# New ranks for the planned order of a three-stage float32 kernel, and softmax two blocks ahead in place of three

## The chip, the cores and the metric

One core of a Trainium2 chip runs the kernel. The metric is the device time of one execution in microseconds. Traces come from a profiled execution of their own.

## The reference

Eight batches (B = 8) of 576 tokens (S) pass through three stages, all in float32:

```
kv  = einsum('bhsd,bhse->bhde', k, v)              # 8 heads of 64
out = einsum('bhsd,bhde->bhse', q, kv)
x   = out / sqrt(mean(out*out, -1) + 1e-6) * g_norm       # (8, 576, 512)
w   = softmax over the top 2 of 4 of x @ w_gate
for e in 4 experts (64 wide):
    a  = softmax(causal(scale * (x @ wq[e]) @ (x @ wk[e]).T))
    y += mask_e * w_e * ((a @ (x @ wv[e])) @ wo[e])
h   = gelu(y @ w_in); u, v = h[..., :512], h[..., 512:]
v_s = einsum('ts,bsd->btd', w_sg, layernorm(v) * g_ln) + b_sg
out = y + (u * v_s) @ w_out
```

Below, "the attention" is the masked softmax attention of the four experts (called heads 0 to 3 in the text). What the kernel calls the first stage (q k v products, norm) feeds it.

## The kernel before, in words

Nearly every product of two float32 operands is made as three fast products: each operand is split in a high part (a rounding, on ScalarE) and a low part (a difference, on VectorE or GpSimd), and high x high, high x low and low x high are summed in PSUM.

The program is written in two phases. Phase 1 (class Phase1, from line 404) handles first stage and attention, batch by batch, and phase 2 (class Phase2, from line 1020) the last stage. Nothing is issued as it is written: a Recorder (line 208) keeps each operation with its tiles. Its plan (line 289) then walks a model of the five engines, and whenever an engine of the model is free it gives it the operation with the lowest number in the record, among those whose operands are ready and whose buffers are to be had. trace (line 377) issues everything in the order of the model's start times. So all instructions carry line 395, and the profile's groups are told apart by their tiles. On the chip each engine takes its instructions in that fixed order.

The numbers in the record come from merge (line 1006). Work is cut into streams (generators); each stream has a stretch of ranks, in units of a batch, from OPT["w"] (line 49). A stream's next step has the rank lo + (hi - lo) x (cost of its steps so far) / (its total), and merge always runs the step with the lowest rank. The streams of batch b (streams, line 981), all of them shifted by b:

- front (line 689): for four pairs of heads, kv, outT and stat (tiles kvps, outps, statps), then rstd (line 585; tiles ya, yb, yc, rr), the reciprocal roots.
- norm (normall, line 711): the products nps, the scaled tile o, and its halves xhi and xlo. There is one buffer for xhi and xlo, so norm of a batch follows the last q and k of the batch before.
- v (vpart, line 719): five tiles vps, and the gates (line 666). qk0 and qk1 (qkpart, line 731): q and k of heads 0, 1 and of heads 2, 3 (tiles qkps, hiT, loT); SyncE's DMAs then spread them into qs, kh and kl.
- attn (line 857): 20 blocks (4 heads x 5 row blocks). scores (line 738) makes scps on TensorE, adds the mask and takes the minimum on VectorE, and the exponential on ScalarE (tile prob, 4 buffers). transp (line 787) transposes block n - ahead (tile tps), and splits it into aTh and aTl; av (line 817) is the product with v.
- wts (line 499): 12 splits of the first stage's weights (wstage into whi and wlo), at the start alone.
- conv and conv2 (line 952): the last stage's weights are read, put together, split and stored to DRAM (tiles cv_*, wxps), in 16 + 27 units spread over the batches. Each unit has small operations on ScalarE, VectorE and GpSimd, and DMAs on SyncE's queue.
- u (Phase2.first, line 1229): loads, then the nine raw V tiles (vmat) and the four raw U tiles (upart) of the last stage's first batches (tiles ps, copied to vraw and u by ScalarE and VectorE). Their buffers come free only when all other streams of phase 1 but attn are done.

What follows in Phase2.rest (line 1249) has the highest numbers: vnorm (line 1155: gelu, the layer norm's statistics on VectorE, lny on GpSimd, the scaled tiles vg, vn and vhi), then spart and opart (tiles ps). The PSUM pools have 4 banks for attn and 4 for the rest; ps of V and U have 4.

Keys with _0 hold for batch 0 alone. The loops that the change touches through OPT:

```
def merge(first, others=()):
    live = [[lo, (hi - lo) / total, gen, True] for lo, hi, total, gen in first]
...
        t = min(live, key=lambda u: u[0])
        cost = next(t[2], 0)
...
            t[0] += t[1] * (cost or 1.0)
```

Of the kernel before, what the change touches and what calls it, by code (L numbers as in the profile page):

```python
# [45 lines left out]
HF = 288  # L46
BIG = 1.0e9
SMALL = float(np.array(897 << 20, np.uint32).view(np.float32))
OPT = dict(ob=1, sx=0, pinq=0, dv=0, pin=1, cvb=2, xb=1, ldb=2, hp={}, n1=0, n2=0, f1=0, pa=4, sA=(), dg=0, cost=(1.01, 0.88, 1.22, 1.47, 1.28), avi=1, prb=4, ahb=2, alb=2, qkb=2, ahead=3, w={'attn': (0.0, 1.0), 'qk1': (-0.013, 0.222), 'qk0': (-0.54, -0.204), 'v': (-0.683, -0.28), 'front': (-1.386, -0.923), 'norm': (-0.832, -0.787), 'conv': (0.032, 3.4), 'conv2': (3.4, 7.2), 'wts': (-1.938, -1.368), 'u': (0.25, 1.0), 'front_0': (-1.763, -1.646), 'v_0': (-1.478, -1.291), 'qk0_0': (-1.025, -0.914), 'qk1_0': (-0.003, 0.152), 'norm_0': (-1.6, -1.5)})


AFTER = {
# [351 lines left out]
class Phase1:  # L404
# [6 lines left out]
    def __init__(self, tc, late, early, ins, wts, gvd, nb):  # L411
# [4 lines left out]
        self.ac = right("ac", 1)  # L416
        self.qk = right("qk", OPT["qkb"])
        self.vv = right("vv", 2)
        self.at = right("at", 2)
        self.psa = right("psa", OPT["pa"], space=PSUM)  # L420
        self.cst = left("cst", 1)
        self.ld = left("ld", OPT["ldb"])
        self.xp = left("xp", 1)
        self.tmp = left("tmp", 1)
        self.cv = left("cv", OPT["cvb"])
        self.psp = left("psp", 7 + OPT["sx"] - OPT["pa"], space=PSUM)
        if not OPT["sx"]:
            self.aux = left("aux", 1, space=PSUM)
# [952 lines left out]
```

## Time and profile before

| what | value |
|---|---|
| median of 3 runs | 894.33 us (893.02 to 898.92) |
| the profiled execution, its own time | 893.27 us |
| its span, first to last instruction | 891.5 us |
| TensorE busy with matmuls | 853.2 us, 96% |
| VectorE, ScalarE, GpSimd busy | 512.4, 464.7, 350.8 us |
| mean granted TensorE clock | 0.980 |

Busy times are unions over the span; idle time of an engine is put down to what ended it. A granted clock of 1.00 is 2.4 GHz and 0.50 is 1.2 GHz. All stretches (A:B) are microseconds from the span's start. Phase 1 fills the first 528 us or so, phase 2 the rest.

### The profile page before, as it was taken

Reading aid. Unit: us, or ns where it says so; the run is one execution under the profiler, and the core shown is the slowest. Engines: PE = TensorE matmul, PEld = TensorE weight load, DVE = VectorE, ACT = ScalarE, POOL = GpSimd, SP = SyncE. Lnnn points to the kernel's source line nnn. Section 1 sums busy time; section 2 is a strip of 40 time slices with the busy share of each in tenths; the row PEclk is TensorE's granted clock in tenths of the full one; section 3 lists DMA queues with packets and bytes.
Section 4 is the critical chain, followed back from the end, with each engine's and each line's share of the span. In section 5 each row is a group of like instructions: output and inputs, shape, how many; then the busy total and the mean of one; then the engine's idle time right before and its main releaser. Section 6 shows DMA issues by size and latency. Waiting matters only on the chain.

```text
span 891.5 us, 16825 instructions
## 1 busy us (share of the span) xinstructions
PE 853.2 (96%) x5992; PEld 794.8 (89%) x5992; DVE 512.4 (57%) x1427; ACT 464.7 (52%) x1211; POOL 350.8 (39%) x398
## 2 busy tenths in 40 slices
PE   7799998999999999999999979999999999999998
PEld 4598997988989989988898769999999999999998
DVE  1757677788866787888878765633342423230110
ACT  1556676677766776867767765522242324231110
POOL 0284266485743644768622223313131413130210
PEclk9799998999999999999899989999999999999999
DMA  9378373674864956746435936020202020101011
GB/s 306 133 196 215 95 217 82 194 215 124 228 179 127 254 156 181 213 148 168 132 88 137 315 109 241 26 94 14 94 26 94 14 93 1 54 1 54 14 41 54
DMA packets 76262, 114.34 MB, mean 128 GB/s; under 512 B 12865, under 2 KB 40321, under 8 KB 76178
## 3 DMA queue, kind: packets, MB, share of 16 engines
q1 hardware_dynamic: 75938, 112.87, 43.0%
q8 instruction: 48, 0.79, 0.4%
q0 software_dynamic: 240, 0.39, 0.2%
q14 instruction: 36, 0.29, 0.1%
HBM read 58.14 MB, written 26.77 MB: 95 GB/s over the span
## 4 chain that ended last, share of the span: by engine, by line
PE 86%; DVE 8%; ACT 2%; issue 1%; DMA 1%; SPq 0%; POOL 0%; ACTq 0%; DVEq 0%; POOLq 0%
PE ps L395 42%; PE qkps L395 10%; PE vps L395 7%; PE avps L395 6%; PE scps L395 5%; PE tps L395 4%; PE kvps L395 4%; PE outps L395 3%; PE statps L395 2%; DVE aTl L395 1%; PE wxps L395 1%; DVE prob L395 1%; DVE o L395 1%; PE nps L395 1%; PE rps L395 1%
## 5 line engine op out<-in xcount | busy, mean ns | idle before, releaser
L395 PE MATMUL ps<-wsh,vn 128*128 128x288 f32 x576 | 119.7, 295 | 0.0
L395 ACT ACTIVATE prob<-prob,small 128x128 f32<-128x128 f32 (+4 forms) x160 | 96.6, 605 | 20.5 <-DVE small L395 18.1
L395 POOL TENSOR_TENSOR gl<-g,gh 128x576 fp32r<-128x576 f32 x32 | 45.8, 1432 | 134.3 <-ACT gh L395 134.2
L395 PEld LDWEIGHTS ps<-wsh,vn 128*128 128x128 f32 x576 | 94.3, 188 | 0.6
L395 DVE CUSTOM_DVE_ANT_0 prob<-scps,mask_sb 128x128 f32<-128x128 f32 (+4 forms) x160 | 75.2, 475 | 18.8 <-PE scps L395 17.5
L395 DVE TENSOR_TENSOR aTl<-tps,aTh 128x384 fp32r<-128x384 f32 (+1 forms) x192 | 79.9, 430 | 7.0 <-ACT aTh L395 5.3
L395 DVE TENSOR_TENSOR g<-ps,u 128x288 f32<-128x288 f32 x64 | 29.1, 454 | 86.7 <-PE ps L395 86.7
L395 ACT CAST aTh<-tps 128x384 fp32r<-128x384 f32 (+1 forms) x192 | 69.4, 380 | 17.8 <-PE tps L395 14.2
L395 PE MATMUL qkps<-xhi,whi 128*128 128x288 f32 x256 | 78.4, 306 | 0.1
L395 PE MATMUL tps<-id_sb,prob 96*128 96x96 f32 (+2 forms) x480 | 73.0, 261 | 3.8 <-DVE small L395 1.3
L395 PE MATMUL qkps<-xhi,wlo 128*128 128x288 f32 x256 | 75.8, 296 | 0.0
L395 PE MATMUL qkps<-xlo,whi 128*128 128x288 f32 x256 | 75.7, 296 | 0.0
L395 PE MATMUL ps<-wsl,vn 128*128 128x288 f32 x256 | 75.6, 295 | 0.0
L395 PE MATMUL ps<-gh,wo2l 128*128 128x288 f32 x256 | 75.4, 295 | 0.0
L395 PE MATMUL ps<-gl,wo2h 128*128 128x288 f32 x256 | 75.3, 295 | 0.0
L395 PE MATMUL ps<-gh,wo2h 128*128 128x288 f32 x256 | 75.3, 294 | 0.0
L395 POOL TENSOR_SCALAR lny<-mv 128x1 f32<-128x1 f32 x36 | 22.3, 620 | 131.7 <-DVE mv L395 131.3
L395 PE MATMUL scps<-kh,qs 128*128 128x128 f32 (+2 forms) x192 | 69.7, 368 | 4.4 <-DVE small L395 2.2
L395 POOL TENSOR_TENSOR xlo<-o,xhi 128x576 fp32r<-128x576 f32 x30 | 42.2, 1421 | 58.6 <-ACT xhi L395 58.6
L395 PEld LDWEIGHTS tps<-id_sb,prob 96*128 96x128 f32 (+2 forms) x480 | 52.3, 140 | 12.6 <-DVE small L395 2.2
L395 PE MATMUL avps<-aTh,vst 128*128 128x320 f32 (+4 forms) x224 | 61.8, 296 | 1.8 <-DVE aTl L395 1.3
L395 ACT COPY oev<-ps 128x288 f32<-128x288 f32 x32 | 12.7, 398 | 92.8 <-PE ps L395 92.8
(169 smaller groups left out, 2629.1 us busy)
## 6 DMA issues: line engine op xcount, KB each, us to landing
kv<-in_kvp SPq DMA_DIRECT2D x30, 384.0 KB, 5.1
kh<-hiT SPq DMA_DIRECT2D x64, 144.0 KB, 3.2
kl<-loT SPq DMA_DIRECT2D x64, 144.0 KB, 3.1
out<-oev SPq DMA_DIRECT2D x32, 288.0 KB, 2.1
q<-in_qT SPq DMA_DIRECT2D x30, 288.0 KB, 4.5
kv<-in_kvp SPq DMA_DIRECT2D x30, 192.0 KB, 5.2
qs<-hiT SPq DMA_DIRECT2D x32, 144.0 KB, 2.5
qs<-loT SPq DMA_DIRECT2D x32, 144.0 KB, 2.6
```

Source lines behind the costliest of these rows:

```text
L395: f(*[val(v) for v in op.args], **{k: val(v) for k, v in op.kw.items()})
```

## The change

Only the table of options is changed: the ranks w of most streams, and ahead, the number of blocks by which scores runs before transp. No operation is added or removed.

```diff
-OPT = dict(... ahead=3, w={'attn': (0.0, 1.0), 'qk1': (-0.013, 0.222), 'qk0': (-0.54, -0.204), 'v': (-0.683, -0.28), 'front': (-1.386, -0.923), 'norm': (-0.832, -0.787), 'conv': (0.032, 3.4), 'conv2': (3.4, 7.2), 'wts': (-1.938, -1.368), 'u': (0.25, 1.0), 'front_0': (-1.763, -1.646), 'v_0': (-1.478, -1.291), 'qk0_0': (-1.025, -0.914), 'qk1_0': (-0.003, 0.152), 'norm_0': (-1.6, -1.5)})
+OPT = dict(... ahead=2, w={'attn': (0.056, 1.056), 'qk1': (-0.013, 0.222), 'qk0': (-0.655, -0.127), 'v': (-0.716, -0.324), 'front': (-1.368, -0.958), 'norm': (-0.847, -0.775), 'conv': (-0.519, 3.449), 'conv2': (3.4, 7.2), 'wts': (-1.735, -1.411), 'u': (0.831, 1.9), 'front_0': (-1.854, -1.661), 'v_0': (-1.499, -1.126), 'qk0_0': (-1.283, -1.172), 'qk1_0': (0.042, 0.197), 'norm_0': (-1.6, -1.5)})
```

The ranks of u are counted from batch 7: 7.25 to 8.0 before, 7.831 to 8.9 after.

## Rows read from the trace of the kernel before

**Rows 1.** The page: TensorE's busy time, its busy tenths in 40 slices, its transposes

```profile
PE 853.2 (96%) x5992; PEld 794.8 (89%) x5992; DVE 512.4 (57%) x1427; ACT 464.7 (52%) x1211; POOL 350.8 (39%) x398
...
PE   7799998999999999999999979999999999999998
...
L395 PE MATMUL tps<-id_sb,prob 96*128 96x96 f32 (+2 forms) x480 | 73.0, 261 | 3.8 <-DVE small L395 1.3
```

**Rows 2.** Stretches: length, busy us (instructions) of PE, PEld, DVE, ACT, POOL; clock; DMA

```profile
25.50:35.50 10.00, 5.00 (x19) 3.40 (x19) 9.79 (x26) 5.90 (x17) 0.79 (x1) 0.76 0.41 146
...
512.50:528.10 15.60, 9.32 (x70) 8.37 (x68) 13.39 (x28) 10.34 (x21) 4.18 (x8) 0.92 0.35 109
528.10:541.00 12.90, 12.89 (x82) 12.89 (x83) 1.33 (x2) 10.33 (x23) 2.17 (x3) 0.83 0.66 234
```

**Rows 3.** Stretches of seven troughs, last q, k matmul to first v matmul of batches 1 to 7

```profile
70.60:86.20 15.60, 14.00 (x96) 11.90 (x95) 13.75 (x40) 11.12 (x32) 5.81 (x6) 1.00 0.90 229
132.50:148.20 15.70, 13.63 (x67) 11.27 (x66) 12.36 (x36) 10.55 (x29) 9.31 (x9) 0.78 0.41 108
197.80:207.40 9.60, 9.16 (x51) 7.04 (x49) 8.71 (x25) 7.25 (x20) 3.11 (x3) 1.00 0.75 188
260.20:266.40 6.20, 5.60 (x34) 3.98 (x33) 5.59 (x16) 4.84 (x16) 2.98 (x3) 0.98 0.68 163
316.40:330.10 13.70, 12.14 (x83) 9.68 (x81) 13.13 (x38) 9.91 (x32) 4.88 (x4) 1.00 0.70 187
373.40:387.40 14.00, 13.08 (x85) 9.92 (x83) 12.89 (x40) 12.16 (x36) 7.85 (x8) 1.00 0.72 207
431.40:440.10 8.70, 6.58 (x30) 4.65 (x29) 8.56 (x24) 7.44 (x23) 2.23 (x3) 0.81 0.66 166
```

**Rows 4.** Stretches at half clock: two in troughs, one behind the raw U tiles

```profile
139.90:146.70 6.80, 6.13 (x25) 5.88 (x26) 4.54 (x16) 3.29 (x7) 4.62 (x6) 0.50 0.14 49
...
436.80:443.60 6.80, 6.80 (x27) 6.09 (x27) 5.59 (x17) 4.88 (x11) 5.73 (x6) 0.50 0.45 116
525.60:532.40 6.80, 4.29 (x18) 4.29 (x19) 2.34 (x5) 3.88 (x9) 3.87 (x6) 0.50 0.09 36
```

**Rows 5.** Timeline of VectorE between batch 0's statistics and its norm

```profile
27.68 1.08 DVE L395 SCALAR_TENSOR_TENSOR wlo<-wstage,whi 128x256 fp32r<-128x256 f32 x3
28.68 0.44 DVE L395 SCALAR_TENSOR_TENSOR yb<-yc,yb 16x288 f32<-16x288 f32 x1
```

**Rows 6.** Timeline of TensorE: waits for rr (batches 0, 1, 7) and for u

```profile
31.37 1.32 PE L395 MATMUL nps<-rr,bsel_sb 80*128 80x288 f32 x3 [4.52 <-DVE rr L395]
...
81.19 0.37 PE L395 MATMUL nps<-rr,bsel_sb 80*128 80x288 f32 x1 [0.74 <-DVE rr L395]
...
436.56 0.65 PE L395 MATMUL nps<-rr,bsel_sb 80*128 80x288 f32 x2 [0.38 <-DVE rr L395]
...
528.11 0.61 PE L395 MATMUL ps<-xh,wih 128*128 128x288 f32 x1 [5.91 <-ACT u L395]
```

**Rows 7.** Timeline of ScalarE while TensorE waits for u

```profile
522.37 0.72 ACT L395 ACTIVATE vn<-vg,lny 128x512 fp32r<-128x512 f32 x1 [1.96 <-DVE vg L395]
...
526.40 0.72 ACT L395 ACTIVATE vhi<-vg,lny 128x512 fp32r<-128x512 f32 x1 [1.61 <-POOL lny L395]
```

**Rows 8.** ScalarE's exponentials and TensorE's transposes: the second block and the last of 160

```profile
62.36 0.50 ACT L395 ACTIVATE prob<-prob,small 128x256 f32<-128x256 f32 x1
...
65.50 0.27 PE L395 MATMUL tps<-id_sb,prob 128*128 128x128 f32 x1
...
67.52 0.27 PE L395 MATMUL tps<-id_sb,prob 128*128 128x128 f32 x1
...
501.47 0.78 ACT L395 ACTIVATE prob<-prob,small 96x576 f32<-96x576 f32 x1 [0.53 <-DVE small L395]
...
514.34 1.04 PE L395 MATMUL tps<-id_sb,prob 128*128 128x128 f32 x10
```

**Rows 9.** The conversions' two-input operation on VectorE: ns min/median/max

```profile
L395 DVE SCALAR_TENSOR_TENSOR cv_h<-cv_w,cv_x x24: 408/476/1643, 37.1 to 443.9; 128x256 uint32<-128x256 uint32 x24
```

More of the change, by code (lines that the diff above doesn't have):

```diff
@@ L48 @@
 SMALL = float(np.array(897 << 20, np.uint32).view(np.float32))
-OPT = dict(ob=1, sx=0, pinq=0, dv=0, pin=1, cvb=2, xb=1, ldb=2, hp={}, n1=0, n2=0, f1=0, pa=4, sA=(), dg=0, cost=(1.01, 0.88, 1.22, 1.47, 1.28), avi=1, prb=4, ahb=2, alb=2, qkb=2, ahead=3, w={'attn': (0.0, 1.0), 'qk1': (-0.013, 0.222), 'qk0': (-0.54, -0.204), 'v': (-0.683, -0.28), 'front': (-1.386, -0.923), 'norm': (-0.832, -0.787), 'conv': (0.032, 3.4), 'conv2': (3.4, 7.2), 'wts': (-1.938, -1.368), 'u': (0.25, 1.0), 'front_0': (-1.763, -1.646), 'v_0': (-1.478, -1.291), 'qk0_0': (-1.025, -0.914), 'qk1_0': (-0.003, 0.152), 'norm_0': (-1.6, -1.5)})
+OPT = dict(ob=1, sx=0, pinq=0, dv=0, pin=1, cvb=2, xb=1, ldb=2, hp={}, n1=0, n2=0, f1=0, pa=4, sA=(), dg=0, cost=(1.01, 0.88, 1.22, 1.47, 1.28), avi=1, prb=4, ahb=2, alb=2, qkb=2, ahead=2, w={'attn': (0.056, 1.056), 'qk1': (-0.013, 0.222), 'qk0': (-0.655, -0.127), 'v': (-0.716, -0.324), 'front': (-1.368, -0.958), 'norm': (-0.847, -0.775), 'conv': (-0.519, 3.449), 'conv2': (3.4, 7.2), 'wts': (-1.735, -1.411), 'u': (0.831, 1.9), 'front_0': (-1.854, -1.661), 'v_0': (-1.499, -1.126), 'qk0_0': (-1.283, -1.172), 'qk1_0': (0.042, 0.197), 'norm_0': (-1.6, -1.5)})
 AFTER = {
```

## The prediction

> **What bounds the kernel now.** Read the page first: TensorE is busy 96% of the span, and in 40 slices the first two, the seventh, the 24th (513 to 535 us) and the last alone fall under nine tenths [rows 1]. The program's matmuls are the same before and after, so the change can only take away (or add) TensorE's idle time and the stretches in which its clock is at 1.2 GHz. Second view: the waits of TensorE and the gaps in its timeline. They leave three places. (a) The start: TensorE sits idle 4.52 us until rr of batch 0 is there [rows 6], in a stretch in which VectorE is busy 9.79 of 10 us [rows 2]. (b) Seven troughs, one per batch from batch 1: the last q and k of a batch are through, the next batch's norm isn't, and TensorE has the attention alone. Summed over the seven stretches, 83.5 us, its idle time is 9.3 us [rows 3]; in two of them the clock falls to half for 6.8 us [rows 4]. (c) The joint of the phases: 6.28 us idle between 512.5 and 528.1 us [rows 2], nearly all of it one wait of 5.91 us for ScalarE's copies of u [rows 6], with a fall of the clock behind it [rows 4]. From there to the last slices TensorE is full [rows 1], and no rank alters that.
>
> **The change part by part.** The sum is made against the profiled execution's 893.3 us (span 891.5 plus 1.8 around it), which lies 1.1 under the median of the runs, 894.3.
>
> *Weights and front of batch 0.* By the formula of ranks, rstd of batch 0 stood at -1.763 + 0.117 x 8.9/9.4 = -1.652, behind 7 of the 12 weight splits (a split each 0.0475 from -1.938). Now it stands at -1.671, behind 3 (each 0.027 from -1.735). The row of VectorE shows what a split costs there: three wlo, 1.08 us, stand between two steps of the way to rr [rows 5], so one costs 0.36. Four splits fewer ahead of rstd are 4 x 0.36 = 1.4 us of VectorE; ScalarE's half of a split may add as much. But an engine of the model doesn't leave a split half done, and its gaps will still be filled with them, so I take 1.0. The splits that are pushed back come due before q and k, behind the v products. Ends: 0 and -2.8. v_0 is stretched, and q and k of batch 0 are put among its last tiles: the order of matmuls changes, not their sum. Zero, covered by the front of batch 1; without that cover one v tile.
>
> *Front, norm, v, q and k of the later batches, and the attention 0.056 later.* The end of front (rstd) moves from b - 0.948 to b - 0.980, while the last q and k of the batch before keep their ranks. A batch lasts (436.56 - 81.19)/6 = 59.2 us by the first nps of batches 1 and 7 [rows 6], so rr is asked for 0.032 x 59.2 = 1.9 us sooner. There is use for it: nps follows the end of q and k by 10.6 us in batch 1 and by 5.2 us in batch 7 (436.56 less 431.4, the left edge of that stretch) [rows 3, 6], in the mean of seven by 4.6. TensorE idles 9.3/83.5 = 0.11 us per us of trough, so 7 x 1.9 us less of trough is worth 1.5 us. The halved clock costs (6.13 + 6.80)/2 = 6.5 us in its two long stretches [rows 4]; troughs 16% shorter would give back 1.0 of it. That is 2.5; I take 2.0, since one trough has no such lag (nps there comes 0.6 us behind q and k). Ends: all 9.3 + 6.5 = 15.8 us gained, or, with two troughs more at half clock and idle time up by a third, 2 x 3.4 + 3.1 = 9.9 lost. The attention moves later against everything else, which only hands it more of the filling.
>
> *Softmax two blocks ahead.* A block has one step less between its scores and its transposes. In rows: the second block's exponential ends at 62.86 and its transposes start at 67.52, a slack of 4.7 us; had they started with those of the block before, at 65.50, 2.6 would be left. For the last block the exponential ends at 502.25, and the last transposes come from 514.34 on [rows 8]. From these two to each other, over all 152 neighbours within a batch, the median left is 2.3 us, the tenth percentile 0.47, and only three, all in batch 7, go below zero, by 0.3 us in sum. I take +0.3. Ends: 0 and +5, if the model plans a third of 152 blocks 0.1 us too tight. No buffer is won: four prob buffers stay.
>
> *Conversions.* 115 steps now run from -0.519 instead of 0.032, at 0.0345 each instead of 0.0293. By rank 1.0 that is 44 steps instead of 33, one or two units more beside batch 0, and as many fewer beside batches 1 and 2. Each unit issues its reads and its stores on SyncE's queue, ahead of q, k and kv moves that are ready later: a unit that waits there holds them up. TensorE has matmuls of the front to do meanwhile, so I cost it at +0.4; ends 0 and +4 (two units, 2 us of late q or k each).
> The conversions' operation with two inputs takes 408 ns at best, 476 in the median and 1643 at most [rows 9]. The Trainium skill (SBUF — State Buffer, "SBUF: two separate sides") says why it may: VectorE with two SBUF inputs and a GpSimd operation that reads SBUF share a pair of ports under an exclusive lock, and who comes second waits. It speaks against putting conversions beside VectorE's busiest batch. By it two units more would add 2 x 1.2 = 2.5 us of VectorE there, and the sum would be some 2 us higher; the row's median says that it seldom happens.
>
> *Raw U and V.* Before, V's nine tiles ranked 7.27 to 7.70 and U's 7.75 to 7.94, among heads 2 and 3 of batch 7 (their scores 7.39 to 7.82, the last av 7.96). Now V ranks 7.86 to 8.47 and U 8.54 to 8.81, and the last av 8.02: all but two tiles stand behind the attention. As filling they can start no earlier, since their buffers and loads set that. But the tail of the attention (the last transposes from 514.34 on [rows 8]) no longer comes between V and U, and neither do its copies on ScalarE and VectorE. That tail is what put vnorm ahead of U's copies: ScalarE waited 1.96 and 1.61 us inside vnorm [rows 7], with TensorE's banks full of finished U tiles, and the copies came only behind it, which let TensorE on at 528.11 [rows 6]. With U straight behind V, a copy is ready after every 6 matmuls and outranks vnorm. From 512.5 on TensorE loses 6.28 us idle [rows 2] and 4.29/2 = 2.1 to the clock [rows 4], 8.4 in all; I take 6.0, since the chain over GpSimd stays on ScalarE's queue. Ends: 0 and -8.4. Next in line is vnorm of the first five tiles, due before spart; TensorE has the rest of U and the second batch's U to cover it, most of the 12.9 us of matmuls in 528.1 to 541.0 [rows 2].
>
> Sum: 893.3 - 1.0 - 2.0 + 0.3 + 0.4 - 6.0 = **885.0 us**.
>
> **The rivals.**
> (1) *The troughs' falls go as well.* If rr is there when q and k end, both long falls (6.5) and half of the idle time (4.6) vanish in place of the 2.0: 885.0 - 9.1 = 876 us. For it: four of the seven troughs have no fall already. Against it: VectorE is busy 75.0 of their 83.5 us [rows 3], and moving ranks takes nothing off it.
> (2) *Little happens.* The model gives a free engine whatever is ready, so ranks only settle ties, and ScalarE's wait in the joint moves to another copy. The start's 1.0 and a third of the joint's 6.0 remain: 890 us. For it: the troughs lag by latency, not by rank. Against it: the joint's order was plainly set by the tail between V and U.
> (3) *Slower: the troughs run dry.* With transposes a block earlier and the front sooner, TensorE goes into a trough with one block less in hand: 73.0/160 = 0.46 us of transposes each [rows 1], 3.2 us over seven, and where that tips the clock, 3.4 us more. It decides from three new falls on. With all five troughs that keep their clock now falling, and the joint's gain halved: 893.3 - 1.0 - 3.0 + 3.2 + 5 x 3.4 = 909; with three, 903. For it: two troughs fall already. Against it: shorter troughs, and the attention 0.056 later has more to give, not less.
>
> **How the numbers follow.** About 1% is what a measurement of this kernel can tell from no change: faster means under 885.4. Chances: the forecast 0.46 (its own range 881 to 889), rival 1 0.17, rival 2 0.25, rival 3 0.12. Half of the forecast and nearly all of rival 1 make faster 0.40; rival 2, the other half and the milder part of rival 3 make the same 0.49; slower keeps 0.11. The range takes in the forecast, rival 2 and most of rivals 1 and 3: 873 to 902.
>
> **What would show it.** Right: nps of batch 0 before 30.9 us; the wait for u under 2 us and no V tile between the attention's last blocks; the sum of the troughs' idle time under 8 us; waits of tps for prob not above 2 us. Wrong: ScalarE still waiting inside vnorm with u uncopied; a clock fall in a trough that has none now; SyncE holding q, k or kv behind cv_ moves while TensorE idles.

## The result, and the profile after

The changed kernel takes 873.46 us (median of 4 runs, 870.64 to 875.77), the kernel before 894.65 us (4 runs, 893.02 to 898.92): a ratio of 0.9751 [0.9712, 0.9789], 2.5% faster. 885.0 us had been forecast. The profiled execution, the slowest of the four, took 875.77 us, 17.5 us less than that of before; its span is 874.0 us.

The page of the changed kernel, which answers to [rows 1]:

```profile
PE 848.6 (97%) x5992; PEld 794.6 (91%) x5992; DVE 508.4 (58%) x1427; ACT 464.4 (53%) x1211; POOL 352.4 (40%) x398
...
PE   7699999999999999999999999999999999999998
...
L395 PE MATMUL tps<-id_sb,prob 96*128 96x96 f32 (+2 forms) x480 | 74.6, 263 | 1.6 <-DVE aTl L395 0.6
```

The instructions are the same in number. The low slice at the joint (the 24th of before) is gone. TensorE's busy time is lower too, by 4.6 us, though its matmuls are the same: that doesn't fit a gain of idle time alone, and it comes back below.

Where the 17.5 us of the two profiled executions lie is read from four marks, the first nps of batches 0, 1 and 7 and the end of the span. To the first nps of batch 0: 31.37 to 30.48 us, -0.9. From there to batch 1: 49.8 to 50.4, +0.6. From batch 1 to batch 7: 355.4 to 342.1, -13.3. From batch 7 to the end: 454.9 to 451.0, -3.9.

The last two stretches in the kernel before (columns as in rows 2):

```profile
81.20:436.60 355.40, 343.87 (x2479) 314.68 (x2479) 280.50 (x857) 252.44 (x723) 205.20 (x223) 0.99 0.61 170
...
436.60:891.50 454.90, 441.28 (x3122) 425.36 (x3122) 189.03 (x440) 173.49 (x378) 114.33 (x130) 0.98 0.24 79
```

and in the changed kernel:

```profile
80.90:423.00 342.10, 337.61 (x2466) 314.25 (x2464) 271.28 (x845) 248.37 (x713) 204.84 (x221) 0.98 0.62 175
...
423.00:874.00 451.00, 443.05 (x3140) 425.37 (x3140) 194.00 (x456) 177.64 (x393) 117.53 (x134) 0.99 0.25 81
```

From batch 1 to 7 the idle time (length less PE's busy time) falls from 11.5 to 4.5 us, 7.0 of the 13.3; the other 6.3 come off the busy time of nearly the same matmuls. Behind the mark of batch 7 the idle time falls from 13.6 to 8.0 us, and 18 matmuls more lie there than before.

The seven troughs, which answer one by one to [rows 3]:

```profile
70.50:89.30 18.80, 17.69 (x104) 14.90 (x104) 15.51 (x50) 13.76 (x40) 7.15 (x6) 0.87 0.66 173
133.50:142.00 8.50, 7.51 (x42) 5.92 (x41) 7.58 (x21) 6.58 (x17) 3.42 (x3) 1.00 0.74 181
193.90:199.00 5.10, 5.10 (x35) 4.45 (x34) 4.64 (x15) 4.26 (x11) 2.80 (x2) 1.00 0.65 159
252.80:256.10 3.30, 3.16 (x20) 2.28 (x18) 3.16 (x10) 2.96 (x7) 2.24 (x2) 1.00 0.61 145
306.00:312.60 6.60, 5.94 (x39) 4.46 (x38) 5.94 (x16) 5.05 (x13) 2.48 (x2) 1.00 0.84 209
362.70:369.80 7.10, 6.65 (x39) 5.02 (x37) 6.91 (x20) 5.26 (x14) 3.06 (x3) 0.86 0.67 193
420.90:426.90 6.00, 5.33 (x24) 3.18 (x22) 5.94 (x19) 5.44 (x15) 2.27 (x3) 0.92 0.61 160
```

Six are shorter and the first is longer. Their sum is 55.4 us against 83.5, their idle time 4.0 against 9.3. Counted from the start of the last q, k matmul to the start of the first v matmul, the measure used for all runs below, it is 57.5 against 85.8.

The stretches at half clock, which answer to [rows 4]:

```profile
84.60:91.40 6.80, 6.26 (x24) 5.28 (x24) 5.89 (x20) 4.89 (x15) 5.76 (x5) 0.50 0.17 44
313.30:316.70 3.40, 3.40 (x16) 3.40 (x15) 1.85 (x7) 1.77 (x8) 2.94 (x3) 0.50 0.70 212
367.90:374.70 6.80, 6.64 (x26) 5.95 (x27) 4.17 (x15) 3.46 (x11) 5.95 (x5) 0.50 0.84 210
425.90:432.70 6.80, 6.79 (x29) 6.59 (x30) 4.52 (x14) 3.64 (x11) 5.04 (x4) 0.50 0.59 152
```

Three long ones begin in troughs (1, 6 and 7), where before it was two (2 and 7). The long ones in trough 2 and at the joint are gone; troughs 1 and 6, which had none, have one. Before, there was also a short one at the end of trough 4:

```profile
266.10:269.60 3.50, 3.40 (x15) 3.22 (x16) 2.67 (x10) 2.37 (x6) 3.47 (x3) 0.51 0.92 273
```

Between the marks of batches 1 and 7 that makes 17.0 us at half clock where it was 10.2: there the clock gave nothing back, it took more.

The start and the joint, from the timeline, beside [rows 5 to 7]:

```profile
27.46 0.41 DVE L395 SCALAR_TENSOR_TENSOR wlo<-wstage,whi 128x256 fp32r<-128x256 f32 x1
27.80 0.44 DVE L395 SCALAR_TENSOR_TENSOR yb<-yc,yb 16x288 f32<-16x288 f32 x1
...
30.48 0.85 PE L395 MATMUL nps<-rr,bsel_sb 80*128 80x288 f32 x2 [4.51 <-DVE rr L395]
...
507.44 0.29 PE L395 MATMUL ps<-xh,wih 128*128 128x288 f32 x1
...
511.36 0.72 ACT L395 ACTIVATE vn<-vg,lny 128x512 fp32r<-128x512 f32 x1 [0.59 <-DVE vg L395]
511.98 0.38 ACT L395 COPY u<-ps 128x288 f32<-128x288 f32 x1
512.42 0.40 PE L395 MATMUL ps<-xh,wih 128*128 128x288 f32 x1 [1.48 <-ACT u L395]
```

At the start one split stands between these two steps of rstd where three stood; ahead of rr VectorE makes nine of the twelve, where it made eleven. At the joint the wait for u is 1.48 us where it was 5.91. V's nine tiles run as filling among the attention's last blocks (482.7 to 507.6 us; the last av starts at 505.8), U starts straight behind them at 507.44, and ScalarE still goes through its share of vnorm before it copies u.

### The profile page after: what moved, and what is told of

It is laid out like the page before. It is cut to its first block, busy times and chain, and to the rows that moved or that the text cites. A ratio compares the mean times of both kernels' runs of the same rounds, so it can differ in the third digit from the quotient of the medians.

```text
span 874.0 us, 16886 instructions
## 1 busy us (share of the span) xinstructions
PE 848.6 (97%) x5992; PEld 794.6 (91%) x5992; DVE 508.4 (58%) x1427; ACT 464.4 (53%) x1211; POOL 352.4 (40%) x398
## 4 chain that ended last, share of the span: by engine, by line
PE 92%; DVE 5%; ACT 1%; issue 1%; DMA 1%; SPq 0%; POOL 0%; DVEq 0%; ACTq 0%
PE ps L395 42%; PE qkps L395 11%; PE vps L395 7%; PE scps L395 6%; PE avps L395 6%; PE tps L395 5%; PE kvps L395 4%; PE outps L395 4%; PE statps L395 2%; PE wxps L395 2%; PE nps L395 2%; DVE o L395 1%; PE rps L395 1%; DMA q<-in_qT 1%; DVE prob L395 1%
## 5 line engine op out<-in xcount | busy, mean ns | idle before, releaser
L395 PEld LDWEIGHTS tps<-id_sb,prob 96*128 96x128 f32 (+2 forms) x480 | 55.2, 142 | 10.6 <-ACT prob L395 1.9
```

The source lines that it names most:

```text
L395: f(*[val(v) for v in op.args], **{k: val(v) for k, v in op.kw.items()})
```

## The experiments

Theory A: the gain from batch 1 to 7 is the chain of the troughs. rr and norm come sooner, each us is worth far more than TensorE's idle share, and each part has a price of its own. Theory B: every set of ranks makes the planner draw another order, and the orders differ by about 1% whatever the part was meant to do; the changed kernel is then a good draw. Prices below are differences of ratios times 894.65 us; the intervals are 0.5 to 1% wide, 4 to 9 us. Each kernel's ratio is to the kernel before in runs beside it (medians of 894.1 to 895.9 us).

Each run also lists its span and its mean granted clock. Span x (1 - clock) is an estimate of what the halved clock cost that run: it counts half of the time at half clock as lost (in u3 below, 27 matmuls in 6.8 us, against 402 in the other 57.0 us of that batch). For the kernel before it is 17.6 to 18.9 us on five chips, for the changed one 15.0. The last two columns split the difference from the kernel before, as means over all runs, into what is left at full clock (span x clock) and this part of the clock's. They are good to about 2 us.

| run | median us | ratio to before | nps 1 to 7 | nps 7 to end | troughs | wait for u | at full clock | the clock's |
|---|---|---|---|---|---|---|---|---|
| before | 894.65 | 1 | 355.4 | 454.9 | 85.8 | 5.9 | 0 | 0 |
| changed kernel | 873.46 | 0.9751 [0.9712, 0.9789] | 342.1 | 451.0 | 57.5 | 1.5 | -18.5 | -3.5 |
| u1_ahead3 | 876.07 | 0.9796 [0.9771, 0.9821] | 337.2 | 457.9 | 50.3 | 6.1 | -14.6 | -3.2 |
| u2_old_batch | 882.46 | 0.9863 [0.9837, 0.9889] | 347.1 | 452.1 | 68.4 | 3.1 | -9.0 | -3.1 |
| u3_old_conv | 880.82 | 0.9846 [0.9824, 0.9868] | 349.3 | 451.1 | 51.7 | 1.8 | -14.1 | +0.9 |
| u4_old_u | 883.16 | 0.9865 [0.9836, 0.9894] | 338.9 | 460.3 | 56.5 | 7.1 | -11.6 | 0.0 |
| a1_ahead2 | 892.84 | 0.9956 [0.9926, 0.9986] | 351.0 | 454.5 | 79.2 | 0.7 | -3.4 | -0.4 |
| a2_new_batch | 881.38 | 0.9844 [0.9813, 0.9875] | 343.5 | 454.5 | 46.3 | 4.1 | -8.3 | -6.5 |
| a3_new_conv | 896.49 | 1.0005 [0.9977, 1.0033] | 354.1 | 459.4 | 75.2 | 5.9 | -4.4 | +4.8 |
| a4_new_u | 895.70 | 1.0010 [0.9988, 1.0031] | 355.0 | 454.1 | 86.6 | 4.7 | -0.7 | +0.2 |
| b1_front_norm | 895.07 | 1.0003 [0.9980, 1.0026] | 355.2 | 456.0 | 76.2 | 5.9 | -0.7 | +1.3 |
| b2_v_qk0 | 899.47 | 1.0049 [1.0023, 1.0074] | 356.4 | 455.9 | 82.1 | 5.9 | +2.1 | +2.1 |
| b3_attn | 892.24 | 0.9973 [0.9949, 0.9997] | 351.5 | 458.0 | 66.8 | 7.5 | -4.1 | +1.9 |
| c1_front_norm_attn | 896.28 | 1.0019 [0.9992, 1.0046] | 356.2 | 456.8 | 72.7 | 7.3 | -2.1 | +3.9 |
| c2_v_qk0_attn | 886.03 | 0.9904 [0.9873, 0.9935] | 346.3 | 452.7 | 61.4 | 0.7 | -8.6 | -0.5 |
| n1_probe | 905.31 | 1.0103 [1.0075, 1.0130] | 363.1 | 456.6 | 90.3 | 5.9 | +2.0 | +8.1 |
| p1_probe_new | 884.84 | 0.9895 [0.9858, 0.9933] | 347.0 | 455.8 | 61.0 | 5.0 | -13.0 | +2.9 |
| c3_ahead_3_2 | 878.00 | 0.9808 [0.9765, 0.9850] | 338.0 | 458.3 | 51.6 | 6.1 | -14.1 | -3.7 |
| c4_front_sooner | 882.96 | 0.9874 [0.9837, 0.9911] | 345.5 | 457.2 | 59.8 | 5.0 | -13.3 | +1.0 |
| d1_late_rr | 883.61 | 0.9899 [0.9848, 0.9951] | 349.0 | 449.9 | 65.2 | 1.5 | -12.9 | +2.5 |

The four columns behind the ratio are us of the one profiled execution, the last two us against the kernel before (for the changed kernel, against its mean on the five chips). Below, the middle is the stretch from the first nps of batch 1 to that of batch 7.

### One part of the changed kernel undone

u1_ahead3: `-ahead=2` `+ahead=3`.

> The changed kernel with scores three blocks ahead again. The changed kernel stood at 873.5 us, 21 under the one before; 13 of these lie between the norm of batch 1 and that of batch 7. Theory L (lookahead: with two blocks ahead the softmax no longer crowds VectorE and ScalarE while a norm is due): 884 or more, with the seven troughs back near 83 us in sum. Theory R (the batch streams' ranks, the front sooner above all): 873 to 876, troughs as in the changed kernel, 55 us. Theory C (conversions sooner): 873 to 876. Theory N (no part in particular, any other set of ranks gives another order and lands within some 10 us): 876 to 886.

u2_old_batch, the five ranks of the later batches as before:

```diff
-'attn': (0.056, 1.056), 'qk0': (-0.655, -0.127), 'v': (-0.716, -0.324), 'front': (-1.368, -0.958), 'norm': (-0.847, -0.775)
+'attn': (0.0, 1.0), 'qk0': (-0.54, -0.204), 'v': (-0.683, -0.28), 'front': (-1.386, -0.923), 'norm': (-0.832, -0.787)
```

> The changed kernel with the old ranks of front, norm, v, qk0 and attn, all else changed. Theory R: 884 or more, rr of batches 3 to 7 late again by some 2 us and the troughs 75 us or more. Theory L: 873 to 877. Theory C: 873 to 877. Theory N: 876 to 886.

u3_old_conv: `-'conv': (-0.519, 3.449)` `+'conv': (0.032, 3.4)`.

> The changed kernel with the conversions' old ranks. Theory C: 880 to 884, the loss between the norms of batches 2 and 3, 65 us again in place of 58. Theories R and L: 872 to 876. Theory N: 876 to 886.

u4_old_u: `-'u': (0.831, 1.9)` `+'u': (0.25, 1.0)`.

> The changed kernel with the old ranks of the raw U and V. The prediction's step on the joint: 878 to 880, TensorE waits 4 us or more for ScalarE's copies of u, with the attention's last transposes between V and U. Theory N for the joint (the wait moves with any change): no more than 2 us either way, 872 to 876.

Each part undone costs time: 4 (within the intervals), 10, 8.5 and 10 us, 33 in sum, where the whole change brought 22. Prices that belong to the parts and add up would not exceed the whole. The excess is no proof, since the changed kernel's own interval stands in each of the four: by the intervals it could be nothing. At full clock the parts cost 3.9, 9.5, 4.4 and 6.9 us undone, 24.7 in sum, where the whole brought 18.5. Nor do all losses lie where the part has its place. u3 differs in the conversions and has shorter troughs than the changed kernel (51.7 against 57.5), and yet loses 7.2 us between batches 1 and 7. It loses them in one batch, from the nps of batch 3 to that of batch 4 (63.8 us against 56.2), and 3.4 of the 7.6 are a fall of the clock that the changed kernel doesn't have there:

```profile
191.50:255.30 63.80, 62.71 (x429) 57.77 (x429) 48.97 (x154) 44.53 (x128) 40.32 (x45) 0.95 0.61 171
195.70:202.50 6.80, 6.80 (x27) 6.07 (x28) 5.16 (x18) 4.88 (x13) 6.09 (x6) 0.50 0.71 176
```

With three blocks ahead (u1) the middle is 4.9 us shorter than in the changed kernel and the joint 6.9 longer, with a wait for u of 6.1 us. The shorter middle is the clock's: u1 has 3.4 us at half clock there, the changed kernel 17.0. u4 has the changed kernel's order on every engine up to 478 us, so it also gives the scatter between two executions of one order: 338.9 against 342.1 in the middle, with 6.8 us at half clock against 17.0. Its loss lies in the last stretch, 460.3 against 451.0, where its change is.

### One part alone, on the kernel before

The same edits the other way round: ahead, the five ranks, conv, u.

> The kernel before with two blocks ahead, nothing else. Theory P (the parts are worth what undoing them cost: batch ranks 9, conversions 7, raw U and V 10, lookahead 3): 891. From the places in the trace of the undone lookahead (norm of batch 1 to norm of batch 7: 337 us with three blocks ahead, 342 with two; the joint dearer by 7): the middle 5 us longer than the 355 of the kernel before, the joint some 7 shorter. Theory N (any other set of ranks lands some 10 us off, either way): 884 to 904, with no such split by place.

> The kernel before with the new ranks of front, norm, v, qk0 and attn. Theory P: 885, the gain between the norms of batches 1 and 7 (355 us before, 346 to 350 here), rr 1 to 2 us sooner against the end of q and k in every batch from 3 on. If ranks only help together: 890 to 895. Theory N: 884 to 904.

> The kernel before with the conversions' new ranks. Theory P: 887, the gain between the norms of batches 2 and 4 (125 us before, 118 here). If ranks only help together: 890 to 895. Theory N: 884 to 904.

> The kernel before with the new ranks of raw U and V. Theory P: 884, all of it behind the norm of batch 7 (454.9 us from there to the end before, 445 here), TensorE's wait for u under 2 us. The prediction's own price for this step: 888. If the wait only moves: 891 to 896.

Only the five ranks do much alone (-14 us; in the profiled execution the middle is 11.9 shorter); ahead brings 3.9, the conversions and u nothing that the time shows. Without the clock's part three of the four prices agree with what undoing cost: ahead brings 3.4 us alone (3.9 undone), the five ranks 8.3 (9.5), the conversions 4.4 (4.4). The conversions alone don't show in the time because the clock took 4.8 us more. Only u differs, 0.7 alone and 6.9 undone: by the time it costs 10 us when it is taken out of the changed kernel and brings none when put into the old one. There V's last tiles fall behind the attention (the last av at 514.5 us, U from 522.9), but the wait only shrinks from 5.91 to 4.7 us. And the wait isn't the price: with two blocks ahead alone the wait is nearly gone, as the waits of TensorE show (us in total, times, longest; u is the last line),

```profile
PE avps L395 <- ACT aTh L395: 2.1, 1, 2.1
PE tps L395 <- DVE aTl L395: 1.5, 4, 0.7
PE tps L395 <- ACT prob L395: 1.4, 2, 0.8
...
PE ps L395 <- ACT u L395: 0.7, 1, 0.7
```

but the last stretch is 454.5 us, as before (454.9):

```profile
437.40:891.90 454.50, 444.31 (x3125) 426.68 (x3124) 189.87 (x442) 173.11 (x379) 112.99 (x127) 0.98 0.24 79
```

TensorE is idle 3.4 us less there (10.2 against 13.6) and busy 3.0 us more. The stretch from the nps of batch 0 to that of batch 1 scatters too: a4 has the order of the kernel before up to 498 us, and took 53.5 us for it instead of 49.8, with waits of 4.2 us for the DMAs of q that the other execution doesn't have.

### The five ranks split

On the kernel before: front and norm; v and qk0; attn; the first with attn; the second with attn.

> The kernel before with the new ranks of front and norm alone. The five batch streams together took it to 881.4, the norms of batches 1 and 7 being 343.5 us apart in place of 355.4. Theory F (the prediction's: the front's end 1.9 us sooner against the last q and k is what counts): 882 to 886, rr 1 to 2 us sooner in batches 3, 5, 6 and 7. Theory Q (v, q and k sooner, so that the front's small operations are no longer behind them at the end of q and k): 892 to 896. Theory A (the attention 0.056 later against all preparation, so that the norm's operations go ahead of softmax on VectorE and ScalarE): 892 to 896. Theory N: 886 to 902, whatever the part.

> The kernel before with the new ranks of v and qk0 alone. Theory Q: 882 to 886, norms of batches 1 and 7 some 345 us apart. Theories F and A: 892 to 896. Theory N: 886 to 902.

> The kernel before with the attention's new ranks alone. Theory A: 882 to 886, the time from nps to the first v matmul down from 7.3 us in the mean to 5.5. Theories F and Q: 892 to 896. Theory N: 886 to 902.

> The kernel before with the new ranks of front, norm and attn. Alone, front and norm gave 895.1, attn 892.2, all five streams 881.4. Theory FA (the norm's chain needs the front sooner and the attention later, v and qk0 are beside the point): 880 to 885, troughs 46 to 60 us. Theory QA (the attention later needs v and qk0 sooner): 889 to 894. If all five are needed: 889 to 894.

> The kernel before with the new ranks of v, qk0 and attn. Theory QA: 880 to 885, troughs 46 to 60 us. Theory FA, or all five needed: 889 to 897.

Front and norm, to which the forecast gave its 1.9 us, bring nothing alone (+0.3) nor with attn (+1.7), though their troughs are 9.6 and 13.1 us shorter. v and qk0 alone cost 4.4. attn alone brings 2.4. v, qk0 and attn together bring 8.6, and with front and norm 14. At full clock the two are 8.6 and 8.3: the difference between them is the clock's (-0.5 and -6.5), so front and norm add nothing that can be measured there either. One line divides all runs but one: with the new v, qk0 and attn together the middle is 337 to 349 us, without them 351 to 363. The exception is u2, without them at 347; the gap of some 2 us between the two groups is no wider than the scatter of one order.

### How much an order is worth: two probes

A shift of 0.006 of a batch (0.35 us) that no one would price: v and front later, qk0 sooner, once on each kernel.

```diff
-'qk0': (-0.54, -0.204), 'v': (-0.683, -0.28), 'front': (-1.386, -0.923)
+'qk0': (-0.546, -0.21), 'v': (-0.677, -0.274), 'front': (-1.38, -0.917)
```

> A probe: the kernel before with v and front 0.006 of a batch later and qk0 0.006 sooner, about a third of a microsecond, which no theory gives a meaning. Theories F, Q and A: 893 to 897, as before. Theory N: off by 4 us or more, either way.

> The same probe on the changed kernel: v and front 0.006 of a batch later, qk0 0.006 sooner. Theory N in full (any set of ranks draws its time anew): anything from 873 to 905. Theory G (the new ranks lie in a better region, and their neighbours keep most of the gain; one order differs from the next by some 10 us within it): 873 to 884, with the seven troughs at 50 to 65 us in sum, against 76 to 90 around the kernel before.

It cost 9 us on the kernel before and 13 on the changed one. The probe on the kernel before has these stretches at half clock between batches 1 and 7:

```profile
139.00:149.20 10.20, 9.15 (x37) 8.39 (x37) 6.17 (x19) 4.81 (x13) 6.09 (x6) 0.50 0.00 0
268.70:272.10 3.40, 3.40 (x16) 3.40 (x17) 2.63 (x10) 2.27 (x6) 3.30 (x3) 0.51 0.95 283
326.80:337.00 10.20, 10.15 (x46) 9.37 (x45) 6.57 (x22) 5.67 (x14) 6.82 (x8) 0.50 0.64 171
```

That is 23.8 us where the kernel before had 10.2 in that stretch. With half of it lost, 6.8 of the 7.7 us by which the stretch is longer are falls of the clock, in troughs only 4.5 us longer in sum. The two columns on the right say the same of all runs: in the mean this probe took 10 us more, of which 8.1 are the clock's and 2.0 are left at full clock; for the other, against the changed kernel, it is 6.4 and 5.5. So theory B has this much: a shift without a meaning moves the time by 1%, and a difference of 10 us between two sets of ranks isn't yet a reason. But most of that draw is the clock, and at full clock it is 2 to 6 us. Two other tries at the changed kernel's ranks:

```diff
-        ahead = OPT["ahead"]
+        ahead = 3 if b < self.nb - 1 else OPT["ahead"]
```

> The changed kernel with three blocks ahead in batches 0 to 6 and two in batch 7. The trace with three blocks everywhere had 337 us between the norms of batches 1 and 7 (342 in the changed kernel, 339 in one with the same order up to there) but lost 7 at the joint. If the two halves are independent: 868 to 872, TensorE's wait for u under 2 us. If the joint's order hangs on what comes before it: 873 to 880.

and `-'front': (-1.368, -0.958)` `+'front': (-1.398, -0.988)`.

> The changed kernel with front 0.03 of a batch sooner still. Theory T with ranks that steer it (rr sooner makes troughs shorter and the time with them): 866 to 872, troughs under 52 us. Theory G (a neighbour like any other): 876 to 885.

Both have higher medians than the changed kernel (by 5 us, at the edge of the intervals, and by 11). The first keeps u1's short middle (338.0) and loses the joint, its wait for u 6.1 us although batch 7 runs two ahead. A front 0.03 sooner still made the troughs no shorter (59.8). Of all kernels run, the changed one has the lowest median; by the intervals u1 can't be told from it, and c3 hardly.

### The chain delayed at a fixed order

Here no rank is touched. Behind the plan, when the operation that writes rr is issued, four idle operations on its input go ahead of it. The order of everything else stays as in the changed kernel.

```diff
+            if op.eng == "vector" and op.fn == "tensor_tensor" and op.args[0].tile.kw.get("name") == "rr":
+                y = val(op.args[1])
+                for _ in range(4):
+                    tc.nc.vector.tensor_scalar(y, y, 1.0, None, op0=OP.mult)
```

> The changed kernel with its order kept, and four more multiplications by 1 on VectorE (16 x 288, 0.45 us each) put in front of each of the eight steps that finish rr, unknown to the planner: rr 1.8 us later in every batch. Theory T (a trough's length costs time, about half of it: kernels with 20 us less of troughs had some 10 us less between the norms of batches 1 and 7): 2 at the start, 5 to 8 in the seven troughs, 880 to 883. If troughs are a symptom and TensorE has enough else to do: 2 to 3 at the start alone, 875 to 877.

The timeline shows the delay in batch 5:

```profile
310.37 1.29 DVE L397 TENSOR_SCALAR ya<-ya 16x288 f32<-16x288 f32 x4
311.69 0.45 DVE L399 TENSOR_TENSOR rr<-ya,rr 16x288 fp32r<-16x288 f32 x1
...
312.28 0.37 PE L399 MATMUL nps<-rr,bsel_sb 80*128 80x288 f32 x1 [0.64 <-DVE rr L399]
```

and the stretch from the nps of batch 1 to that of batch 7 reads:

```profile
81.60:430.60 349.00, 340.69 (x2463) 314.98 (x2462) 278.09 (x871) 248.73 (x715) 205.87 (x222) 0.97 0.62 172
```

The chain to rr is 1.3 us longer in each batch (the four take 0.30 us each, not the 0.45 expected), and nps follows the last q and k by 3.3 us in the mean instead of 2.5. From batch 1 to 7 that is 6 x 1.3 = 7.8 us of delay, and the stretch grew by 6.9: 3.8 of it idle time and 3.1 busy time, with 20.5 us at half clock instead of 17.0. The 0.88 us per us of these two executions is rough, since one order scatters by 3.2 us there.

The runs give it better. For 8 x 1.3 = 10.4 us of delay the time grew by 10 us by the medians and 13 by the ratios; by the two columns 5.6 us of it are at full clock and 6.0 the clock's. That is half a us per us, and as much again through the clock. Not separated is what the 1.3 us cost as lateness and what as VectorE's time, and the planner didn't know of the delay: it is a price at a fixed order, not what a planner gains when the chain is sooner. The one run that keeps the order thus gives theory A a price, well above the tenth of a us of the forecast.

## Why the prediction was wrong in size

The direction was right, and the time lies at the lower end of the range. The terms in turn:

**Start, -1.0.** It measured -0.9 (nps at 30.48, under the 30.9 that was asked for). One pair of executions can't carry that: u4, with the same order, has 29.4. But the eight kernels with the new ranks of the start and no delay have a mean of 30.4, the eleven with the old ones 31.4. The mechanism was the one named, fewer splits ahead of rr, but two fewer and not four: the trace has eleven and nine where the formula of ranks gave seven and three. TensorE's own wait stayed at 4.5 us, since it too came free sooner.

**Troughs, -2.0.** This is the step that failed, with -13.3 us between batches 1 and 7 in place of -2.0. It was "TensorE idles 9.3/83.5 = 0.11 us per us of trough, so 7 x 1.9 us less of trough is worth 1.5 us". Both factors were too small. The length: by the timeline norm followed the last q and k by 2.5 us in the mean (start to start) instead of 4.9, so it came 2.4 us sooner (1.9 had been forecast), but the first v also followed norm 1.6 us sooner (5.7 instead of 7.3), which no step had. That makes 7 x 4.0 = 28.3 us of trough less instead of 13.3. The price: 13.3/28.3 = 0.47 us per us, where the forecast's 2.0 for 13.3 us is 0.15. TensorE's idle share undercounts, since its rows overlap. The timeline of TensorE in the kernel before, at the norm of batch 5:

```profile
320.60 0.30 PE L395 MATMUL scps<-kl,qs 128*96 128x288 f32 x1
320.73 0.30 PE L395 MATMUL nps<-rr,bsel_sb 80*128 80x288 f32 x1
321.15 0.34 PE L395 MATMUL scps<-kh,qs 128*96 128x288 f32 x1
321.33 0.29 PE L395 MATMUL scps<-kl,qs 128*96 128x288 f32 x1
```

A row is 0.30 us long, and the next starts 0.13 us behind it when nothing holds it (320.60 to 320.73). From 320.73 to 321.15 TensorE paused for nearly 0.3 us, and 0.12 of it shows as idle. Count it from start to start, against the pace of the same pair of products (tiles and shapes) in both traces: its 15th percentile, at full clock only. The stretch from batch 1 to 7 then has 223 pauses of over 60 ns before and 163 after, and what is hidden in busy rows falls from 33.5 to 26.9 us, beside the shown idle time. That, with 13 matmuls fewer in the stretch, is how busy time could fall by 6.3 us. Falls of the clock, which were to give back 1.0, took an estimated 3.4 more (half of 17.0 - 10.2).

Over the 20 profiled executions of all kernels, the stretch from batch 1 to 7, less half of its time at half clock, goes with the sum of the troughs: a straight line gives 0.41 us per us and leaves a scatter of 2.6 us. The time at half clock, 3.4 to 25.0 us, doesn't go with that sum. That is a correlation, but the price is about what the delayed chain cost at full clock; what the clock takes comes on top, and what decides it is not shown.

What made the troughs shorter is only partly shown. The forecast's own source, front sooner, brought nothing alone. The new ranks of v, qk0 and attn, which had no term in the sum (the attention's "only hands it more of the filling"), brought 8.6 together. Why these three make better orders isn't settled, nor why u2 does nearly as well without them. By the time alone, troughs and middle don't go in step: c1 has 13.1 us less of trough and 0.8 us more time, but also 20.5 us at half clock instead of 10.2.

**Softmax two blocks ahead, +0.3.** The waits of transposes in the changed kernel were as small as forecast (tps; us in total, times, longest):

```profile
PE nps L395 <- DVE o L395: 2.9, 10, 0.5
PE ps L395 <- ACT u L395: 1.5, 1, 1.5
PE tps L395 <- DVE aTl L395: 0.6, 2, 0.4
PE tps L395 <- DVE small L395: 0.4, 1, 0.4
PE tps L395 <- ACT prob L395: 0.2, 1, 0.2
```

But it isn't +0.3: undone it costs 4 us (within the intervals; 3.9 at full clock), alone it brings 3.9 (3.4). In the changed kernel the loss shows at the joint, where the forecast had looked for nothing; alone the gain doesn't lie there. Where it comes from is open.

**Conversions, +0.4.** The sign was wrong. At full clock they bring 4.4 us, alone and in the changed kernel; alone the clock took that back (+4.8), in the changed kernel undoing them cost 8.5 with the clock's part. What u3 loses lies in one batch far behind the place where a queue was feared. The row of the two-input operation on VectorE came out better, not worse:

```profile
L395 DVE SCALAR_TENSOR_TENSOR cv_h<-cv_w,cv_x x24: 408/426/1617, 39.0 to 441.6; 128x256 uint32<-128x256 uint32 x24
```

The median was 476 ns in [rows 9]. The 2 us that the prediction worked out beside the rule of the Trainium skill (SBUF — State Buffer, "SBUF: two separate sides") don't show; whether the long ones, up to 1617 ns, waited for that lock is not shown.

**Raw U and V, -6.0.** The stretch from batch 7 to the end gained 3.9 us with 18 matmuls more in it, the wait for u 4.4, and the fall of the clock at 525.6 is gone. The picture was half right: U follows straight behind V and the wait is under 2 us, but "no V tile between the attention's last blocks" was wrong, V fills there. And ScalarE still waits inside vnorm ahead of U's copies, a sign named as against. The move needs the rest of the change: nothing alone, 10 us in company (6.9 at full clock).

**The rivals.** The time is that of rival 1 (876), but not by its mechanism: the long falls in troughs didn't vanish but became three, with new ones in troughs 1 and 6: a fall in a trough that had none had been named as a sign against. That the number came near is luck. Rival 2 ("ranks only settle ties") is refuted by the result; the probes add that even ties move 1%. Of rival 3 came two new falls, with the troughs shorter and not drier.

**What no sum could give.** The seven other kernels that keep most of the new ranks (u1 to u4, c3, c4, p1) lie between 876.1 and 884.8 us, 881.2 in the mean, all above the changed kernel (u1 and c3 not clear of the noise). By that mean, an estimate that takes the four with a part undone as neighbours, some 13 of the 21 us belong to the new ranks as a group, and 8 to the one order that they happen to give. At full clock the three nearest (c3, c4, p1) stand 4 to 5.5 us above the changed kernel, so its draw is worth about that much there. The kernel before is no bad draw: the eight without the new v, qk0 and attn together (a1, a3, a4, b1 to b3, c1, n1) have a mean of 896.7. The forecast of 885.0 stood 4 us from the group, 11.5 from the draw.

## What to carry to other kernels

Price a stretch in which an engine waits for a chain by delaying that chain at a fixed order, or by counting pauses from start to start, and not by the engine's idle share: here the share gave 0.11 us per us, the delay 0.5 at full clock and about 1 with the clock's part. Take the clock's part out of a comparison before you read the rest (span x granted clock, from every run): here it was most of what a meaningless shift moved, and without it three of four parts had one price, alone and undone. Where a list scheduler draws the order from ranks, shift a rank by a hair first and see how far the time moves; a part's price below that spread (here 1%) isn't shown by the time alone, and one part that brings nothing alone was worth 10 us in company. What one draw wins says little about the next.

## What had not been expected of the hardware

A busy row of TensorE hides pauses: with nearly the same matmuls (13 fewer of 2479) its busy time from batch 1 to 7 fell by 6.3 us while, by estimate, 3.4 us more were lost to the clock. And the clock falls not only in the longest troughs. In the changed kernel it fell in troughs of 7.1 and 6.0 us and kept its level in one of 8.5; one order run twice had 17.0 and 6.8 us at half clock in six batches, and took 342.1 and 338.9 us for them.
